# Unseen quarters left out of the scores on both PSUM banks, with a mask that clips first

## The chip, the cores and the metric

The kernel runs on one core of one Trainium2 chip. The metric is the device time of one execution in microseconds; three executions of the kernel before took 304.59, 306.55 and 308.75 us. Differences under 2% are called the same.

## The reference

Attention with a sliding window and a distance penalty (ALiBi), followed by a normalised two-layer MLP with a residual.

```python
# q, k, v: (8, 8, 576, 64) fp32
scores = q @ k.T / sqrt(64) - slope[h] * |i - j|      # slope[h] = 2 ** -(h + 1), 8 heads
mask   = (i - j >= 0) & (i - j < 128)                 # else -1e9
x      = softmax(scores) @ v                          # -> (8, 576, 512)
xn     = (x - mean(x)) / sqrt(var(x) + 1e-6) * g_ln
out    = x + relu(xn @ w_ch1) @ w_ch2                 # w_ch1 512x2048, w_ch2 2048x512
```

## The kernel before

**Tiling.** The eight batches are taken in four pairs p; a pair has nine blocks of 128 queries: blocks 0 to 7 are four blocks of each batch in turn, block 8 (T) holds the last 64 queries of both batches. That makes 36 blocks, numbered n = 9p + blk. The blocks are put into groups (four of 2 blocks, then seven of 4), and a group goes through the MLP at once.

**Attention of a block.** With a window of 128, a block of 128 queries sees its own keys and the 128 keys before them, `keys = [blk - 2, blk]`. `attend` (L472) does this for four heads at a time (`hps`, two pairs of heads), or for all eight where there is one block of keys. It multiplies in 64x64 tiles of TensorE: for each pair of heads and each block of keys, two halves of the keys (`c`) and two heads (`j`), 16 matmuls of up to 128 query columns (L498). ScalarE takes the exponential from PSUM into `probs` in 16 bits (L509); VectorE multiplies `probs` by a table `m_full` (or `m_ends`, `m_tail`) that holds the decay by distance and is zero outside of the window (`masks`, L531). The scores of a block are not shifted by their maximum.

**Unseen quarters.** Queries stand in PSUM with the even ones first, and half of the queries see none of one half of the keys' tile in a block: a quarter of the tile's columns is outside of the window. `seen` (L446) lists the column ranges to be multiplied: all of them if `all_of_it` (`full`), or in the first pair of batches for blocks under `SEEN` = 8; otherwise without the quarters, and for T only one batch's half (64 columns). Columns that are left out keep what the bank held, and the exponential runs over them too; the table's zeros then take them away.

**Banks.** Scores go to two PSUM places `ps_sc[0]` and `ps_sc[1]`, of two banks each. From block 12 on (`ONE_GO`) the two attends of a block are issued in one go, first onto `ps_sc[1]`, then onto `ps_sc[0]`. `values_at_once` (L586) writes the weighted values of a block, and the sums of its weights, into `ps_sc[1]` too. The sums come from a column of ones behind the values in `vext`. VectorE takes their reciprocal (L602) and multiplies (L603). In the kernel before, an attend onto `ps_sc[1]` from block 12 on has `full` set.

**The order of the work.** The order is written out by hand. `steps` is a list of small pieces of attention work; `weave_at` lets the MLP's units run and puts a given number of steps behind given units. All engines keep program order. From block 12 on a block has four steps: `go` (the two attends of block n + 2, with the exponential of the second put off), the masks that are left over, the values of block n and their centring (L635), then the put-off exponentials, then the masks of block n + 2 and the squares.

**The MLP.** `mlp1` (L858) has 16 units of four matmuls (L868) into one of four `ps_mm` banks; a Relu on ScalarE (L884), or for two of the units on VectorE (L876), writes the hidden tile. From group 4 on the second layer is `mlp2_seven` (L1085): seven products of half size in place of eight (Strassen's scheme), whose operands are sums of hidden tiles made on VectorE (`sum_hidden`, L1066; the subtractions stand on L918). It uses three banks x, t and y. Its products are issued in this order, each (L1098) with what VectorE or ScalarE then does:

| product | then |
|---|---|
| x, from the hidden tile | ScalarE copies x to t |
| y, from the first sum | `onto` the output (L1119) |
| onto x, from the second sum | `onto` (twice, for two blocks) |
| onto t, from the hidden tile | `onto` |
| onto x, from the third sum | `onto`; the product must wait until the `onto` before has read x |
| onto y, from the fourth sum | `onto`, store |
| onto x, from the hidden tile | `onto`, store |

The first sum is finished, the second made and the fourth begun while these run; VectorE does them between the masks and the values' normalising, in the order of the units.

**Loads** come on POOL's queue in the order of a list that `load_until` follows; stores and the transposing DMAs stand on SP's queue.

Of the kernel before, what the change touches and what calls it, by code (L numbers as in the profile page):

```python
# [14 lines left out]
ALU = mybir.AluOpType  # L15
# [14 lines left out]

FIRST_GROUPS, FIRST = 2, 4

BY_DMA = SEEN = 8

IN_HASTE = 10, 11

# [59 lines left out]
def kernel(  # L96
# [10 lines left out]
    nc = tc.nc  # L107
    B, H, S, D = q.shape
# [332 lines left out]
    weights_of, unmasked, scored, scored_only = {}, {}, [], []  # L441

    def in_halves(t):
        return t if len(t.shape) == 3 else t.rearrange("p (r c) -> p r c", r=2)

    def seen(p, blk, o, t, all_of_it):  # L446


        both, every = slice(0, 2), slice(0, HALF)
        first, second = slice(0, HALF // 2), slice(HALF // 2, HALF)  # L450
        if all_of_it or p == 0 and blk < SEEN:
            return [(0, both, every), (1, both, every)]
        if blk == T:
            batches = [slice(0, 1), slice(1, 2)]
            return [(c, batches[c if o == T else t], every) for c in range(2)]
        if o == blk:
            return [(0, both, every), (1, both, second)]
        return [(1, both, every), (0, both, first)]
# [10 lines left out]
                skip_group_check=True,  # L469
            )  # L470

    def attend(p, blk, keys, mask, tag, hps, sc=None, full=False, put_off=False):  # L472

        heads = slice(2 * hps[0], 2 * hps[-1] + 2)
        nk = len(keys)
        if hps[0] == 0:  # L480
            pr = probs_pool.tile([P, H, nk, P], FP16, tag=tag, name=tag)
            for t, o in enumerate(keys):
                weights_of.setdefault((p, blk), []).append((pr, t, o))
        else:
            pr = weights_of[p, blk][-1][0]
        banks = ps_sc[len(scored) % 2 if sc is None else sc]
        scored.append((p, blk))
        ps = banks.rearrange("p j (n t q) -> p j n t q", n=len(hps), t=nk)
        added = p == 0 and blk < ADDED
        qt, b = turned["q", p, blk // 2], blk % 2  # L490
        for n, hp in enumerate(hps):
            for t, o in enumerate(keys):
                kt = turned["k", p, o // 2][:, o % 2]
                for c, r, queries in seen(p, blk, o, t, full):
                    cols = slice(c * HALF, (c + 1) * HALF)
                    for j in range(2):
                        rows = slice(j * HALF, (j + 1) * HALF)
                        nc.tensor.matmul(  # L498
                            in_halves(ps[cols, j, n, t, :])[:, r, queries],
                            kt[rows, hp, cols],  # L500
                            in_halves(qt[rows, b, hp])[:, r, queries],
                            start=not added,
                            stop=True,
                            skip_group_check=added,
                        )
        dst = pr[:, heads].rearrange("p h t q -> p h (t q)")

        def weights():
            nc.scalar.activation(  # L509
                out=dst.rearrange("p (n j) q -> p j n q", j=2),  # L510
                in_=ps.rearrange("p j n t q -> p j n (t q)"),
                func=AF.Exp,
                scale=inv_sqrt_d,
            )

        if put_off:
            scored_only.append(weights)
        else:
            weights()
        if not added:  # L520
            unmasked.setdefault((p, blk), []).append((dst, mask[:, heads, :]))

    def exps():

# [2 lines left out]

    def masks(p, blk, n=3):
        todo = unmasked.get((p, blk), [])
        for dst, mask in todo[:n]:  # L530
            nc.vector.tensor_tensor(out=dst, in0=dst, in1=mask, op=ALU.mult)  # L531
        del todo[:n]

# [16 lines left out]
    def scores_tail(p):  # L550
        attend(*tail_attend(p))
# [3 lines left out]
    def values(p, blk, hg):  # L555

        if hg == 0:
            xs[p, blk] = x_pool.tile([P, DM], FP16, tag="x", name="x")
            sums[p, blk] = small.tile([P, 2], FP32, tag="sum", name="sum")
        ps = ps_mm.tile([P, 4, D + 1], FP32, tag="mm", name="ps_pv")  # L560
        terms = weights_of[p, blk]
        for i in range(4):
            h = 4 * hg + i
            for n, (pr, t, o) in enumerate(terms):
                nc.tensor.matmul(  # L565
                    ps[:, i, :],
                    pr[:, h, t, :],
                    vext[(p * NSLOT + o) % NV][:, h, :],
                    start=(n == 0),
                    stop=(n == len(terms) - 1),  # L570
                )
        rec = small.tile([P, 4], FP32, tag="rec", name="rec")
        nc.vector.reciprocal(out=rec, in_=ps[:, :, D])
        nc.vector.scalar_tensor_tensor(
            out=xs[p, blk][:, hg * 4 * D : (hg + 1) * 4 * D].rearrange(
                "p (h d) -> p h d", h=4
            ),
            in0=ps[:, :, 0:D],
            scalar=1.0,
            in1=rec.unsqueeze(2).broadcast_to([P, 4, D]),  # L580
            op0=ALU.mult,
            op1=ALU.mult,
            accum_out=sums[p, blk][:, hg : hg + 1],
        )

    def values_at_once(p, blk, sc=0):  # L586

        x = xs[p, blk] = x_pool.tile([P, DM], FP16, tag="x", name="x")
        total = sums[p, blk] = small.tile([P, 2], FP32, tag="sum", name="sum")
        ps = ps_sc[sc].rearrange("p g (h e) -> p (g h) e", h=4)  # L590
        terms = weights_of[p, blk]
        for h in range(H):
            for n, (pr, t, o) in enumerate(terms):
                nc.tensor.matmul(  # L594
                    ps[:, h, 0 : D + 1],
                    pr[:, h, t, :],
                    vext[(p * NSLOT + o) % NV][:, h, :],
                    start=(n == 0),
                    stop=(n == len(terms) - 1),
                )  # L600
        rec = small.tile([P, H], FP32, tag="rec8", name="rec8")
        nc.vector.reciprocal(out=rec, in_=ps[:, :, D])  # L602
        nc.vector.scalar_tensor_tensor(  # L603
            out=x.rearrange("p (h d) -> p h d", h=H),
            in0=ps[:, :, 0:D],
            scalar=1.0,
            in1=rec.unsqueeze(2).broadcast_to([P, H, D]),
            op0=ALU.mult,
            op1=ALU.mult,
            accum_out=total[:, 0:1],  # L610
        )
# [5 lines left out]
    def centre(p, blk):  # L617

        total = sums.pop((p, blk))
        mean = small.tile([P, 1], FP32, tag="mean", name="mean")  # L620
        if FIRST <= p * NSLOT + blk < BY_DMA:
            nc.vector.tensor_scalar(
# [17 lines left out]
        if at == 0:  # L640
            turned_x[g] = group_pool.tile([P, NKB, 4 * P], FP16, tag="xT", name="xT")
        if n < BY_DMA or g >= SEVEN:
            centred[p, blk] = xc
        if n >= BY_DMA and n not in IN_HASTE:
            nc.sync.dma_start_transpose(
# [72 lines left out]
    for g, size in enumerate(GROUPS):  # L718
        n = sum(GROUPS[:g])
# [20 lines left out]
    def x_step(n, copy=nc.vector.tensor_copy):  # L740
        return [(turn_x,) + home[n] + order[n] + (copy,)] if n < BY_DMA or n in IN_HASTE else []

# [44 lines left out]
    for n in range(8, ONE_GO):  # L787
        ahead = place[min(n + AHEAD, count - 1)]
        todo = []
# [12 lines left out]
        for tag, m in (("q", n + 5), ("k", n + 6)):  # L802
            if m < count and order[m][1] % 2 == 0 and by_dma(*order[m]):
                p, blk = order[m]
# [4 lines left out]
        steps += [step, second, third, fourth]  # L809

    for n in range(ONE_GO, count):
        todo = []
        if n + 1 < count and order[n + 1][1] == T:
            todo.append(tail_attend(order[n][0]))
        if n + 2 < count:
            todo += attends(*order[n + 2])
        first_of, pairs = n == ONE_GO, (1, 0) if len(todo) > 1 else (0,)
        go = [(attend, *a, sc, first_of or sc == 1, sc == 0) for a, sc in zip(todo, pairs)]  # L820
        step = [(load_until, place[min(n + AHEAD, count - 1)]), (masks,) + order[n]]
        step += [(values_at_once, *order[n], 1), (centre,) + order[n]]

        rest = [(masks, *args[:2], 1) for args in todo]
        rest += [(square, m) for m in {1: (), 3: (n - 2, n)}.get(n % 4, (n,))]
        for tag, m in (("q", n + 5), ("k", n + 6)):
            if m < count and order[m][1] % 2 == 0:
                p, blk = order[m]
                (step if first_of else rest).append((turn_natural, tag, p, blk // 2))
        steps += [go, step, [(exps,)], rest]  # L830
# [456 lines left out]
    for n, vx in enumerate(vext):  # L1287
        if n == 2:
            nc.vector.memset(ones, 1.0)
        nc.vector.memset(vx[:, :, D : D + 1], 1.0)  # L1290
    nc.vector.memset(magic, 0x5F3759DF)
    engine = mybir.EngineType
    with tc.manual_schedule(engines={engine.PE}):
# [64 lines left out]
```

## Time and profile before

| | |
|---|---|
| three executions | 304.59, 306.55, 308.75 us |
| the profiled one | 304.59 us; span from first to last instruction 302.8 us |
| granted TensorE clock, mean | 0.994 |
| TensorE matmuls | 294.7 us busy, 97% of the span, 3778 instructions |
| VectorE | 232.3 us, 77% |
| ScalarE | 184.4 us, 61% |
| GpSimd (loads) | 113.8 us, 38% |
| scores matmuls, L498 | 1088; 768 of 128 columns, 320 of 64 |
| masks, L531 | 66 of 128x1024 |

Busy time of TensorE counts overlapping, pipelined matmuls, so it is read together with the starts of the instructions. A row of instructions has the start in the span, the busy time, engine, line, operation, tiles written and read, shapes and count; in brackets the idle time before it and what ended that. A row of a group has busy time and mean of one in ns, then the idle time before, by what ended it. The chain of waits goes back from the last instruction to whatever released each; a row there has start, time, and engine, tile and line.

### The profile page before, as it was taken

How to read it: one execution, taken by the hardware profiler on the slowest of the kernel's cores; microseconds unless marked ns; L12 is line 12 of the kernel's file. 1: busy time of each engine (PE TensorE's matmuls, PEld its weight loads, DVE VectorE, ACT ScalarE, POOL GpSimd, SP SyncE). 2: the span in 40 equal slices, each digit the busy share in tenths (PEclk: the TensorE clock that was granted, in tenths of full speed). 3: DMA queues.
4: the chain of work that ended last, by engine and by line, in shares of the span. 5: the costliest groups of instructions: out<-in, count | busy, mean ns of one | idle time of the engine just before them, and what ended most of it. 6: DMA issues, size and time to landing. Idle time of an engine off the chain costs nothing.

```text
span 302.8 us, 9262 instructions
## 1 busy us (share of the span) xinstructions
PE 294.7 (97%) x3778; PEld 201.8 (67%) x3778; DVE 232.3 (77%) x616; ACT 184.4 (61%) x338; POOL 113.8 (38%) x153
## 2 busy tenths in 40 slices
PE   7899999999999999999999999999999999999994
PEld 2477755866855478556865686568656865788883
DVE  2588778779886788658866887687888888878983
ACT  5587777868967883478457745674577446606500
POOL 8933756973855571685007171760000000000000
PEclk9799999999999999999999999999999999999999
DMA  9999999999999999999979999999581153006014
GB/s 93 171 199 202 193 158 162 190 136 125 139 122 173 163 128 157 179 194 125 142 125 134 161 105 159 148 145 110 101 131 35 21 99 77 19 19 139 3 35 104
DMA packets 150074, 38.03 MB, mean 126 GB/s; under 512 B 140656, under 2 KB 145920, under 8 KB 150032
## 3 DMA queue, kind: packets, MB, share of 16 engines
q0 software_dynamic: 103792, 18.46, 89.1%
q1 hardware_dynamic: 45760, 18.60, 40.2%
q8 instruction: 29, 0.48, 0.7%
q10 hardware_dynamic: 480, 0.39, 0.5%
q14 instruction: 13, 0.11, 0.1%
HBM read 36.90 MB, written 9.44 MB: 153 GB/s over the span
## 4 chain that ended last, share of the span: by engine, by line
PE 88%; DMA 5%; DVE 3%; ACT 1%; issue 1%; POOL 1%; DVEq 0%; ACTq 0%; POOLq 0%
PE ps_m L868 35%; PE ps_s L1098 22%; PE ps_m L898 9%; PE ps_sc L498 5%; PE ps_sc L594 5%; PE ps_q L1176 4%; PE ps_x L992 3%; DMA q<-q 3%; DMA first<-in_k_dram 2%; PE ps_warm L334 1%; PE ps_tr L346 1%; DVE probs L531 1%; POOL first L190 1%; PE ps_pv L565 1%; PE ps_tx L655 1%
## 5 line engine op out<-in xcount | busy, mean ns | idle before, releaser
L868 PE MATMUL ps_m<-xT,w1g 128*128 128x512 f16 (+1 forms) x512 | 103.9, 353 | 0.2
L884 ACT ACTIVATE ht_all<-ps_m 128x512 f16<-128x512 f32 (+1 forms) x143 | 71.8, 512 | 37.9 <-PE ps_m L868 36.0
L868 PEld LDWEIGHTS <-w1g 128*128 128x128 f16 x512 | 47.6, 98 | 41.7 <-issue 0.6
L509 ACT ACTIVATE probs<-ps_sc 128x1024 f16<-128x1024 f32 x56 | 56.1, 1022 | 9.4 <-PE ps_sc L498 9.4
L289 POOL DMA_DIRECT2D vx<-in_v_dram x40 | 35.3, 893 | 65.1 <-PE ps_sc L594 47.2
L1098 PE MATMUL ps_s<-w,s 128*128 128x256 f16 x384 | 45.7, 273 | 0.1
L1098 PEld LDWEIGHTS <-s 128*128 128x128 f16 x384 | 36.8, 98 | 4.4 <-issue 0.2
L531 DVE TENSOR_TENSOR probs<-probs,m 128x1024 f16<-128x1024 f16 x56 | 36.3, 685 | 1.8 <-ACT probs L509 1.8
L1098 PE MATMUL ps_s<-w,ht_all 128*128 128x256 f16 x288 | 36.1, 273 | 0.0
L679 ACT ACTIVATE junk<-xc 128x512 f16<-128x512 f16 x28 | 17.7, 631 | 26.9 <-DVE xc L635 26.9
L898 PE MATMUL ps_m<-w,ht_all 128*128 128x512 f16 x128 | 31.5, 380 | 0.0
L1098 PEld LDWEIGHTS <-ht_all 128*128 128x128 f16 x288 | 27.3, 98 | 5.0
L278 POOL DMA_DIRECT2D q<-in_q_dram x40 | 27.5, 701 | 6.0 <-DMA vx<-in_v_dram 5.3
L918 DVE TENSOR_TENSOR s<-ht_all 128x1024 f16<-128x1024 f16 (+2 forms) x36 | 20.5, 570 | 11.6 <-ACT ht_all L884 10.6
L498 PEld LDWEIGHTS <-k 64*64 64x64 f16 x1088 | 15.8, 107 | 13.1 <-issue 11.7
L603 DVE SCALAR_TENSOR_TENSOR x<-ps_sc,rec 128x512 f16<-128x512 f32 x32 | 22.1, 692 | 1.2 <-DVE rec L602 0.2
L1119 DVE SCALAR_TENSOR_TENSOR o<-ps_s,rstd,x 128x256 f32<-128x256 f32 x48 | 20.9, 477 | 2.6 <-PE ps_s L1098 2.2
L498 PE MATMUL ps_sc<-q,k 64*64 64x128 f16 (+1 forms) x1088 | 21.6, 213 | 0.9 <-DVE k L420 0.4
L275 POOL DMA_DIRECT2D k<-in_k_dram x20 | 17.9, 911 | 6.1 <-DMA k<-k 4.9
L602 DVE RECIPROCAL rec<-ps_sc 128x8 f32<-128x8 f32 x32 | 6.5, 204 | 17.2 <-PE ps_sc L594 17.2
L594 PEld LDWEIGHTS <-probs 128*128 128x128 f16 x384 | 15.9, 98 | 3.7
L898 PEld LDWEIGHTS <-ht_all 128*128 128x128 f16 x128 | 11.0, 98 | 10.6
(118 smaller groups left out, 377.1 us busy)
## 6 DMA issues: line engine op xcount, KB each, us to landing
out_dram<-o SPq DMA_DIRECT2D x64, 128.0 KB, 3.4
vx<-in_v_dram POOLq DMA_DIRECT2D x32, 128.0 KB, 7.3
w<-in_moe_w_ch_dram POOLq DMA_DIRECT2D x8, 512.0 KB, 11.3
k<-in_k_dram POOLq DMA_DIRECT2D x30, 128.0 KB, 6.9
q<-in_q_dram POOLq DMA_DIRECT2D x48, 64.0 KB, 6.6
q<-in_q_dram POOLq DMA_DIRECT2D x10, 128.0 KB, 6.0
out_dram<-o SPq DMA_DIRECT2D x10, 64.0 KB, 2.0
k<-in_k_dram POOLq DMA_DIRECT2D x8, 64.0 KB, 7.3
```

What stands on the lines that cost most here:

```text
L278: nc.gpsimd.dma_start(out=t[half, b], in_=tokens.rearrange("h (c r) d -> r c h d", r=2)[r],)
L289: nc.gpsimd.dma_start(out=vx[p0 : p0 + n, :, 0:D], in_=v[b, :, t0 : t0 + n, :].rearrange("h p d -> p h d"),)
L498: nc.tensor.matmul(in_halves(ps[cols, j, n, t, :])[:, r, queries], kt[rows, hp, cols], in_halves(qt[rows, b, hp])[:, r, queries], start=no ...
L509: nc.scalar.activation(out=dst.rearrange("p (n j) q -> p j n q", j=2), in_=ps.rearrange("p j n t q -> p j n (t q)"), func=AF.Exp, scale=in ...
L531: nc.vector.tensor_tensor(out=dst, in0=dst, in1=mask, op=ALU.mult)
L594: nc.tensor.matmul(ps[:, h, 0 : D + 1], pr[:, h, t, :], vext[(p * NSLOT + o) % NV][:, h, :], start=(n == 0), stop=(n == len(terms) - 1),)
L603: nc.vector.scalar_tensor_tensor(out=x.rearrange("p (h d) -> p h d", h=H), in0=ps[:, :, 0:D], scalar=1.0, in1=rec.unsqueeze(2).broadcast_t ...
L868: nc.tensor.matmul(ps[:, 0:cols], w[:, kb, fb * P : (fb + 1) * P], xT[:, kb, 0:cols], start=(kb == 0), stop=(kb == NKB - 1),)
L884: nc.scalar.activation(out=ht[:, fb, :], in_=ps[:, 0:cols], func=AF.Relu)
L898: nc.tensor.matmul(sums[at], ht[:, fb, at * P : (at + 1) * P], w2[:, fb, :], start=(fb == 0), stop=(fb == NFB - 1),)
L1098: nc.tensor.matmul(ps[:, pair, :], lhs[:, fb, at : at + P], rhs[:, fb, :], start=(first and pair == 0 and fb == 0), stop=(fb == half - 1), ...
L1119: nc.vector.scalar_tensor_tensor(out=outs[at][:, cols], in0=ps[:, pair], scalar=rstd[:, n : n + 1], in1=(xs[p, blk] if fresh else outs[at] ...
```

## The change

The quarters are left out on `ps_sc[1]` also after values were written there, and in the first pair of batches for blocks 3, 5 and 7. What such a column then holds after the exponential can be past the range of 16 bits (infinite), and infinite times zero is no number; so for these attends (`values_were`) the mask first takes the smaller of the weight and 65504 and then multiplies. The ones behind the values become 2 to the -7, so that the sums left in the bank stay small, and the scaling of the values has the same factor. `full` remains for the one attend on `ps_sc[0]` of block 12's go.

```diff
-BY_DMA = SEEN = 8
+BY_DMA = 8
+ONE = 2.0**-7
+ALL_SEEN = 0, 1, 2, 4, 6
...
-        if all_of_it or p == 0 and blk < SEEN:
+        if all_of_it or p == 0 and blk in ALL_SEEN:
             return [(0, both, every), (1, both, every)]
...
-    def attend(p, blk, keys, mask, tag, hps, sc=None, full=False, put_off=False):
+    def attend(p, blk, keys, mask, tag, hps, sc=None, full=False, put_off=False, values_were=False):
...
-            unmasked.setdefault((p, blk), []).append((dst, mask[:, heads, :]))
+            unmasked.setdefault((p, blk), []).append((dst, mask[:, heads, :], values_were))
...
-        for dst, mask in todo[:n]:
+        for dst, mask, values_were in todo[:n]:
+            if values_were:
+                nc.vector.scalar_tensor_tensor(
+                    out=dst, in0=dst, scalar=65504.0, in1=mask, op0=ALU.min, op1=ALU.mult
+                )
+                continue
             nc.vector.tensor_tensor(out=dst, in0=dst, in1=mask, op=ALU.mult)
...
-            scalar=1.0,
+            scalar=ONE,
...
-        go = [(attend, *a, sc, first_of or sc == 1, sc == 0) for a, sc in zip(todo, pairs)]
+        go = [
+            (attend, *a, sc, first_of and sc == 0, sc == 0, sc == 1) for a, sc in zip(todo, pairs)
+        ]
...
-        nc.vector.memset(vx[:, :, D : D + 1], 1.0)
+        nc.vector.memset(vx[:, :, D : D + 1], ONE)
```

`scalar=ONE` stands in `values` and in `values_at_once`.

More of the change, by code (lines that the diff above doesn't have):

```diff
@@ L605, in values_at_once @@
             in0=ps[:, :, 0:D],
-            scalar=1.0,
+            scalar=ONE,
             in1=rec.unsqueeze(2).broadcast_to([P, H, D]),
```

## The prediction

> **What bounds the kernel now.** I read the page first, then a table by stretches of the span, then the chain of waits, then the rows of TensorE (PE) and VectorE (DVE) one by one around each place where the chain left PE.
>
> ```profile
> span 302.8 us, 9262 instructions
> PE 294.7 (97%) x3778; PEld 201.8 (67%) x3778; DVE 232.3 (77%) x616; ACT 184.4 (61%) x338; POOL 113.8 (38%) x153
> PE 88%; DMA 5%; DVE 3%; ACT 1%; issue 1%; POOL 1%; DVEq 0%; ACTq 0%; POOLq 0%
> core 0: us, PE busy (x) PEld busy (x) DVE busy (x) ACT busy (x) POOL busy (x), PEclk, DMA share, GB/s
> 154.00:185.00 31.00, 31.00 (x373) 20.91 (x372) 23.48 (x61) 19.00 (x31) 12.57 (x16) 1.00 1.46 136
> ```
>
> The first line is the span. The second and third say that the kernel is bound by PE: busy for 97% of the span, and 88% of the chain that ended last lies on it. The stretch 154 to 185 us is one whole group of four blocks: PE is busy throughout at the full clock, DVE for 23.5 of 31 us. DVE looks as if it had a quarter of its time to spare. But 3% of the chain is DVE, and the change puts work on DVE, so the question is where those 3% lie. The chain between 139 and 150 us answers it:
>
> ```profile
> 139.81 0.61 ACT ht_all L884
> 140.42 0.02 issue
> 140.44 0.44 DVE s L918
> ...
> 140.90 0.83 DVE s L918
> 141.73 1.21 DVE probs L531 x2
> 142.93 0.41 DVE s L918
> ...
> 146.20 1.28 DVE probs L531 x2
> 147.48 0.80 DVE o L1119 x2
> 148.28 0.04 issue
> 148.32 1.69 PE ps_s L1098 x14
> ```
>
> When the last Relu of `mlp1` is done (139.81 + 0.61), DVE starts a queue without a gap: two sums of the hidden tile, two masks (`probs` L531), the long sum, the block's normalising (`rec`, `x`), the results `onto` the output, two more masks, and the `onto` that empties bank x. PE's product at L1098, which accumulates into that same bank, waits for that last one and starts 0.04 us after it. Both mask pairs stand inside this queue. So in this stretch each added DVE nanosecond is a PE nanosecond.
>
> **The change, part by part.**
>
> *Matmuls of the scores.* Nothing is added to PE; in the built program 248 matmuls of L498 have 64 columns where they had 128: 21 attends of 16 matmuls have 8 of them halved, and 5 (those of the tail blocks) all 16. The trace has all these forms side by side, since the attend on bank 0 already leaves the quarters out:
>
> ```profile
> 37.46 0.64 PE L498 MATMUL ps_sc<-q,k 64*64 64x128 f16 x32
> 38.03 0.39 PE L898 MATMUL ps_m<-w,ht_all 128*128 128x512 f16 x1
> ...
> 97.41 0.59 PE L498 MATMUL ps_sc<-q,k 64*64 64x128 f16 x32
> 97.94 0.39 PE L868 MATMUL ps_m<-xT,w1g 128*128 128x512 f16 x1
> ...
> 109.58 0.54 PE L498 MATMUL ps_sc<-q,k 64*64 64x128 f16 x32
> 110.05 0.39 PE L1098 MATMUL ps_s<-w,ht_all 128*128 128x256 f16 x2
> ```
>
> From the first matmul of a pair of attends to the next work: full and full, 38.03 - 37.46 = 0.57 us; full and a quarter less, 97.94 - 97.41 = 0.53; full and tail, 110.05 - 109.58 = 0.47. An attend with 8 halved is 0.05 cheaper, a tail one 0.10. In all 21 x 0.05 + 5 x 0.10 = 1.55 us of PE, at the very most.
>
> *Masks.* In the built program 20 of the 66 masks (18 `probs`, 2 `own` with `m_tail`) turn from a TENSOR_TENSOR into a SCALAR_TENSOR_TENSOR with two operations. One in each pair of L531 changes, the first. Nothing else on DVE, ScalarE, POOL or SP moves, and the order of every queue stays. The trace has no SCALAR_TENSOR_TENSOR on 16-bit data of this size, so I bound it by the nearest rows:
>
> ```profile
> L531 DVE TENSOR_TENSOR probs<-probs,m 128x1024 f16<-128x1024 f16 x56 | 36.3, 685 | 1.8 <-ACT probs L509 1.8
> L603 DVE SCALAR_TENSOR_TENSOR x<-ps_sc,rec 128x512 f16<-128x512 f32 x32 | 22.1, 692 | 1.2 <-DVE rec L602 0.2
> L574 DVE SCALAR_TENSOR_TENSOR x<-ps_pv,rec 128x256 f16<-128x256 f32 x8 | 3.4, 424 | 0.3
> L918 DVE TENSOR_TENSOR ps_s<-ps_x,c 128x512 f32<-128x512 f32 x4 | 2.8, 694 | 0.5 <-PE ps_x L992 0.5
> L918 DVE TENSOR_TENSOR s<-ht_all 128x512 f16<-128x512 f16 x10 | 4.3, 425 | 4.8 <-ACT ht_all L884 4.5
> L1119 DVE SCALAR_TENSOR_TENSOR o<-ps_s,rstd,x 128x256 f32<-128x256 f32 x48 | 20.9, 477 | 2.6 <-PE ps_s L1098 2.2
> ```
>
> A TENSOR_TENSOR in 16 bits goes from 425 ns (512 elements) to 685 (1024): 0.51 ns an element. The 32-bit one at 512 takes 694. The SCALAR_TENSOR_TENSOR goes from 424 (256) to 692 (512): 1.05 ns an element, with 156 ns fixed. Low end: the new mask keeps the 16-bit rate, 0.685 us, nothing added. High end: the slope of 1.05 and the fixed part of L1119 (477 - 256 x 1.05 = 208), 1.28 us. I take the rows of the same instruction, 156 + 1024 x 1.05 = 1.23 us, so +0.545 us for each of the 20. The one doubt is that those rows read 32-bit data from PSUM.
>
> [...]
>
> *What of it lies on the path.* In the stages of `mlp1` the added time meets idle time of DVE; the next row after such masks is
>
> ```profile
> 162.39 1.28 DVE L531 TENSOR_TENSOR probs<-probs,m 128x1024 f16<-128x1024 f16 x2
> 163.59 0.68 DVE L918 TENSOR_TENSOR s<-ht_all 128x1024 f16<-128x1024 f16 x1
> 166.12 0.56 DVE L918 TENSOR_TENSOR s<-ht_all 128x768 f16<-128x768 f16 x1 [1.84 <-ACT ht_all L884]
> ...
> 173.50 0.49 PE ps_sc L594 x16
> ```
>
> 1.84 us idle, of which 0.545 is used up: nothing (were that cover gone, 0.545 us late onto the sums). The masked weights themselves are read two blocks later, by the values matmuls at 173.50 (last row, from the chain), so they are never late.
>
> In the second half of each of groups 4 to 8 (`mlp2_seven`) there is no idle time between the last Relu and the emptying of bank x. End of that `onto` against PE's start:
>
> ```profile
> 116.83 0.87 DVE L1119 SCALAR_TENSOR_TENSOR o<-ps_s,rstd,x 128x256 f32<-128x256 f32 x2
> 117.77 0.38 PE L1098 MATMUL ps_s<-w,s 128*128 128x256 f16 x2
> ...
> 177.88 0.87 DVE L1119 SCALAR_TENSOR_TENSOR o<-ps_s,rstd,x 128x256 f32<-128x256 f32 x2
> 178.80 0.38 PE L1098 MATMUL ps_s<-w,s 128*128 128x256 f16 x2
> ...
> 202.72 0.69 DVE L531 TENSOR_TENSOR own<-own,m 128x1024 f16<-128x1024 f16 x1
> 207.88 0.87 DVE L1119 SCALAR_TENSOR_TENSOR o<-ps_s,rstd,x 128x256 f32<-128x256 f32 x2
> 209.19 0.38 PE L1098 MATMUL ps_s<-w,s 128*128 128x256 f16 x2
> ...
> 238.51 0.87 DVE L1119 SCALAR_TENSOR_TENSOR o<-ps_s,rstd,x 128x256 f32<-128x256 f32 x2
> 239.45 0.38 PE L1098 MATMUL ps_s<-w,s 128*128 128x256 f16 x2
> ```
>
> Taking 0.05 us from a DVE end to a PE start, the slack is 0.02 (117.77), none (148.32, where PE already waits), none (178.80), 0.39 (209.19), 0.02 (239.45). Four of these queues hold two changed masks, 2 x 0.545 = 1.09 us; that of 209.19 holds one, because the first place there is an `own` mask of bank 0 that does not change. The stalls: 1.07 + 1.09 + 1.09 + 0.15 + 1.07 = 4.47 us. What is late next: product x with the third sum, and through it the rest of PE's queue. DVE itself recovers behind it, as it next waits for PE there.
>
> *What PE keeps of its saving.* Attends between the last Relu and the waiting product save nothing, for the product starts when DVE says. That is two pairs in each of the five queues: 0.20 (a tail block's two attends) + 0.10 + 0.15 + 0.10 + 0.10 = 0.65 us. Of the six changed attends of the first batches, the two of block 3 and the two of block 5 run just before PE waits for ScalarE's or DVE's results: another 0.20. There remain 1.55 - 0.65 - 0.20 = 0.70 us.
>
> *No cost:* memsets of 2 to the -7 and the constant in the two scalings have the instructions, shapes and places they had.
>
> Sum: +4.47 - 0.70 = +3.8 us against the profiled execution's 304.59 us (span 302.8 and 1.8 around it): 308.4. That execution was the fastest of the three shown; on their median of 306.55 it is 310.3, a ratio of 1.012. I give 310.3.
>
> **The rivals.**
>
> *A. The mask keeps its rate.* If the engine takes two 16-bit results at a time here too, 0.685 us, no queue grows and only the matmuls count: the saving is 0.70, and some 0.15 more in the queue of 209.19, which has slack: 0.85 us less, 305.7. For it: the same operands run at 0.51 ns an element in L531. Against it: each row of this instruction has 1.05. It decides from the mask's duration: nine changed masks stand in the five queues, so the gain of 0.70 is eaten at about 0.08 us each; under 0.77 us the change is not slower.
>
> [...]
>
> *C. The cover in the `mlp1` stages fails too.* DVE also empties two PSUM banks of `mlp1` in each group (L876) in the same queue. If these come late enough for PE to run out of banks, up to two more changed masks per group count: 5 x 2 x 0.545 = +5.5 on top, 316. Against it: the 1.84 us idle above and four banks. It decides from where the idle time behind the masks is below 0.5 us.
>
> *That the matmuls don't shrink* is excluded by the built program and the 0.53 us row.
>
> **How the numbers follow.** Forecast 0.76, A 0.12, B 0.05, C 0.07. The likeliest one's own range: masks from 1.1 to 1.28 us give +2.7 to +4.4, and the three runs shown spread by 2 us to each side: 307.5 to 313. To hold 8 in 10 with A on the low side I give 304.8 to 313.5; B and C are left out. About what a measurement of this kernel can tell from no change is 2%, 6.1 us: 300.4 to 312.7. Over it lie B, C and a small part of the forecast: 0.15; under it hardly anything, since A reaches 305.7: 0.02; within: 0.83.
>
> **What would show it.** In the changed profile: the new form of the mask at about 1230 ns x18; DVE's busy time up by some 11 us to 243; pairs of L498 at 0.47 to 0.48 us before the next work; PE's product at L1098 starting about 1.1 us later behind each last `onto` in four groups; DVE's share of the chain up from 3% to some 10%, all in the second halves of the groups. I am wrong if the mask is at 0.69 us (A) or over 2 us (B), if the five queues got idle time, or if PE waits in the `mlp1` stages for L876 (C).

## The result and the profile after

The changed kernel took 309.63 us (median of six, 308.49 to 310.33) against 306.23 us for the kernel before: a ratio of 1.0107, with a 95% interval of 1.0066 to 1.0149. It is slower by 3.4 us; by the bound of 2% that counts as the same. Medians here and below are of all executions, while ratios and their 95% intervals leave out those more than 1.5% above the fastest of the same kernel, so the two can differ by a few tenths of a percent.

The page of the profiled execution (309.78 us), the lines that answer to those of before:

```profile
span 308.0 us, 9262 instructions
PE 292.9 (95%) x3778; PEld 200.1 (65%) x3778; DVE 244.9 (80%) x616; ACT 184.0 (60%) x338; POOL 112.6 (37%) x153
PE 75%; DVE 12%; DMA 4%; issue 3%; POOL 3%; ACT 1%; DVEq 0%; POOLq 0%
```

DVE has 12.6 us more to do, and its share of the chain that ended last went from 3% to 12%. The 20 longer masks are 10.6 us of that; most of the rest lies in rows that the change does not touch (the centring 13.5 to 14.8 us, the scaled weights `w1g` 4.6 to 5.6). Lines of the file are 12 further down at the end (L1131 is the `onto` that was L1119, L1110 the product that was L1098). The masks, grouped by shape:

```profile
L542 DVE TENSOR_TENSOR probs<-probs,m 128x1024 f16<-128x1024 f16 x38 | 25.4, 685 | 1.6 <-ACT probs L514 1.6
L538 DVE SCALAR_TENSOR_TENSOR probs<-probs,m 128x1024 f16<-128x1024 f16 x18 | 21.9, 1217 | 0.0
```

The clipping mask takes 1217 ns where the plain one takes 685: 0.53 us more. Less the 156 ns that the prediction took as fixed, that is 1.04 ns an element. Next the chain of waits through the second half of one group, to be read beside the chain of before at 139 to 148 us:

```profile
173.46 0.61 ACT ht_all L896
174.06 0.02 issue
174.09 0.44 DVE s L930
...
175.37 1.14 DVE probs L538
176.51 0.60 DVE probs L542
...
180.52 1.13 DVE probs L538
181.65 0.38 DVE probs L542
182.03 0.14 issue
182.18 0.87 DVE o L1131 x2
183.05 0.04 issue
183.09 0.92 PE ps_s L1110 x7
```

From the Relu's end to the product the chain is DVE alone, with a long mask at two places. What PE waited for now, in total, times and longest (the list of waits, PE alone):

```profile
PE ps_s L1110 <- DVE o L1131: 4.4, 4, 1.2
PE ps_m L880 <- DMA w<-in_moe_w_ch_dram: 2.0, 1, 2.0
```

The same product in PE's rows, once for each of the five queues, with the idle time in brackets:

```profile
120.24 0.49 PE L1110 MATMUL ps_s<-w,s 128*128 128x256 f16 x3 [1.08 <-DVE o L1131]
...
151.58 0.60 PE L1110 MATMUL ps_s<-w,s 128*128 128x256 f16 x4 [1.21 <-DVE o L1131]
183.09 0.60 PE L1110 MATMUL ps_s<-w,s 128*128 128x256 f16 x4 [1.13 <-DVE o L1131]
213.52 0.70 PE L1110 MATMUL ps_s<-w,s 128*128 128x256 f16 x5
244.74 0.70 PE L1110 MATMUL ps_s<-w,s 128*128 128x256 f16 x5 [0.97 <-DVE o L1131]
```

Four waits, 4.4 us; the product at 213.52, in the queue with slack, has none. No such line stood in the list of waits before. The second line of the list is a load of weights that landed late at the start. The same matmuls after it, before and in the changed kernel:

```profile
24.54 0.40 PE L655 MATMUL ps_tx<-first_tables,xc 128*128 128x128 f16 x4 [0.47 <-DVE xc L635]
25.78 0.40 PE L666 MATMUL ps_tx<-first_tables,xc 128*128 128x128 f16 x4 [0.52 <-DVE xc L646]
```

So the changed kernel is 1.24 us late there, before any of the waits on DVE. That is the larger part of why the profiled spans differ by 5.2 us and the medians only by 3.4. The other side, PE's saving:

```profile
165.38 0.54 PE L503 MATMUL ps_sc<-q,k 64*64 64x128 f16 x32
165.85 0.82 PE L880 MATMUL ps_m<-xT,w1g 128*128 128x512 f16 x3
```

A pair of attends is past after 0.47 us in place of 0.53.

### The profile page after: what moved, and what is told of

It is laid out like the page before. It is cut to its first block, busy times and chain, and to the rows that moved or that the text cites. A ratio compares the mean times of both kernels' runs of the same rounds, so it can differ in the third digit from the quotient of the medians.

```text
span 308.0 us, 9262 instructions
## 1 busy us (share of the span) xinstructions
PE 292.9 (95%) x3778; PEld 200.1 (65%) x3778; DVE 244.9 (80%) x616; ACT 184.0 (60%) x338; POOL 112.6 (37%) x153
## 4 chain that ended last, share of the span: by engine, by line
PE 75%; DVE 12%; DMA 4%; issue 3%; POOL 3%; ACT 1%; DVEq 0%; POOLq 0%
PE ps_m L880 35%; PE ps_s L1110 13%; PE ps_m L910 9%; PE ps_q L1188 4%; PE ps_sc L605 4%; DMA w<-in_moe_w_ch_dram 3%; PE ps_sc L503 3%; PE ps_x L1004 3%; DVE s L930 3%; DVE probs L538 3%; DVE o L1131 2%; DVE x L614 2%; DVE probs L542 1%; POOL vx L294 1%; ACT ht_all L896 1%
## 5 line engine op out<-in xcount | busy, mean ns | idle before, releaser
L880 PE MATMUL ps_m<-xT,w1g 128*128 128x512 f16 (+1 forms) x512 | 103.9, 353 | 0.3 <-DVE o L1253 0.3
L880 PEld LDWEIGHTS <-w1g 128*128 128x128 f16 x512 | 47.7, 98 | 41.6 <-issue 0.5
L294 POOL DMA_DIRECT2D vx<-in_v_dram x40 | 34.2, 865 | 73.0 <-PE ps_sc L605 61.5
L1110 PE MATMUL ps_s<-w,s 128*128 128x256 f16 x384 | 45.7, 272 | 4.5 <-DVE o L1131 4.4
L1110 PEld LDWEIGHTS <-s 128*128 128x128 f16 x384 | 36.8, 98 | 9.4 <-issue 5.3
L1110 PE MATMUL ps_s<-w,ht_all 128*128 128x256 f16 x288 | 36.1, 273 | 0.0
L1110 PEld LDWEIGHTS <-ht_all 128*128 128x128 f16 x288 | 27.4, 98 | 5.0
L542 DVE TENSOR_TENSOR probs<-probs,m 128x1024 f16<-128x1024 f16 x38 | 25.4, 685 | 1.6 <-ACT probs L514 1.6
L503 PEld LDWEIGHTS <-k 64*64 64x64 f16 x1088 | 14.4, 107 | 13.3 <-issue 11.9
L538 DVE SCALAR_TENSOR_TENSOR probs<-probs,m 128x1024 f16<-128x1024 f16 x18 | 21.9, 1217 | 0.0
L1131 DVE SCALAR_TENSOR_TENSOR o<-ps_s,rstd,x 128x256 f32<-128x256 f32 x48 | 20.5, 476 | 1.2 <-PE ps_s L1110 0.8
L503 PE MATMUL ps_sc<-q,k 64*64 64x128 f16 (+1 forms) x1088 | 20.2, 207 | 1.0 <-issue 0.5
L605 PEld LDWEIGHTS <-probs 128*128 128x128 f16 x384 | 15.9, 98 | 3.7 <-issue 0.2
```

Of the source, the lines that this page charges most:

```text
L294: nc.gpsimd.dma_start(out=vx[p0 : p0 + n, :, 0:D], in_=v[b, :, t0 : t0 + n, :].rearrange("h p d -> p h d"),)
L503: nc.tensor.matmul(in_halves(ps[cols, j, n, t, :])[:, r, queries], kt[rows, hp, cols], in_halves(qt[rows, b, hp])[:, r, queries], start=no ...
L538: nc.vector.scalar_tensor_tensor(out=dst, in0=dst, scalar=65504.0, in1=mask, op0=ALU.min, op1=ALU.mult)
L605: nc.tensor.matmul(ps[:, h, 0 : D + 1], pr[:, h, t, :], vext[(p * NSLOT + o) % NV][:, h, :], start=(n == 0), stop=(n == len(terms) - 1),)
L880: nc.tensor.matmul(ps[:, 0:cols], w[:, kb, fb * P : (fb + 1) * P], xT[:, kb, 0:cols], start=(kb == 0), stop=(kb == NKB - 1),)
L1110: nc.tensor.matmul(ps[:, pair, :], lhs[:, fb, at : at + P], rhs[:, fb, :], start=(first and pair == 0 and fb == 0), stop=(fb == half - 1), ...
```

## The experiments

The theory under test: the change costs the added length of the clipping mask, and only where the mask stands in the queue between the last Relu and the `onto` that empties bank x; the shorter matmuls save a little. Rival 1: the matmuls of 64 columns, or the exponential over values, cost. Rival 2: DVE's load as such costs, wherever it lies. Rival 3 came with the remedy: the wait only moves on to the next bank. The first four kernels split the change into its parts.

**The change with the old mask.** Nothing clips at 65504 here.

```diff
-            if values_were:
+            if False:
```

> The change with the old mask everywhere: quarters left out and the ones at 2 to the -7 as in the change, but every mask a plain TENSOR_TENSOR (no clipping at 65504). Queue theory (what costs is the longer mask where it stands between the last Relu and the emptying of bank x): only the shorter matmuls are left, 0.85 us less than before, some 305.4 us against 306.2; no wait of PE for L1131's onto above 0.2 us. Rival 1 (the cost is in the matmuls of 64 columns, or in the exponential over columns that hold values): stays some 3 us above before. Rival 2 (DVE's total load): as the queue theory here.

Measured: 305.04 us against 306.11, ratio 0.9964 (0.9931 to 0.9998). Rival 1 falls: the part with the matmuls is a gain, and the size forecast (0.85 us would be 0.9972) lies in the interval. The list of waits still has one on the `onto` at L1131, of 0.3 us, a little over the 0.2 us expected. The profiled execution also waited 2.2 us for a transposing DMA (1.6 us in the kernel that clips only outside of the queues, further down); neither the profile before nor that of the changed kernel has this wait, and why it came stays open.

**The mask alone.** All quarters are multiplied, the same 20 masks clip.

```diff
-ALL_SEEN = 0, 1, 2, 4, 6
+ALL_SEEN = 0, 1, 2, 3, 4, 5, 6, 7
...
-            (attend, *a, sc, first_of and sc == 0, sc == 0, sc == 1) for a, sc in zip(todo, pairs)
+            (attend, *a, sc, first_of or sc == 1, sc == 0, sc == 1) for a, sc in zip(todo, pairs)
```

> The other part alone: all quarters multiplied as before, but the same 20 masks clip first. Queue theory: the stalls alone, 4.47 us, so some 310.7 us against 306.2 (ratio 1.0146). Rival 1 (the matmuls cost): within 0.5 us of before. Rival 2 (DVE's total load): +4 us too, not told apart here.

Measured: 310.22 us, ratio 1.0135 (1.0105 to 1.0164), 4.1 us more than before. The mask alone accounts for the whole loss. Its list of waits:

```profile
PE ps_s L1110 <- DVE o L1131: 3.9, 4, 1.1
```

**Clipping only outside of the queues.** The nine masks in the queues don't clip.

```diff
-            if values_were:
+            if values_were and not ((p * NSLOT + blk) % 4 < 2 and mask.shape[1] == 4):
```

> The change, but only the 11 masks outside of the five queues clip (blocks n with n mod 4 = 2 or 3 and the two tails); the nine in the queues are plain. DVE's load is up by 11 x 0.53 = 5.9 us. Queue theory: no stall, 0.85 us less than before, 305.4 us. Rival 2 (each added DVE time costs a like share wherever it stands): 11/20 of 4.2 less 0.85, so 1.5 us more than before, 307.7 us.

Measured: 304.61 us, ratio 0.9950 (0.9926 to 0.9974). "No stall" holds but for one wait on L1131, of 0.4 us at 150.74, in the queue in which PE already waited before the change.

**Clipping only in the queues.** The other eleven don't clip.

```diff
-            if values_were:
+            if values_were and (p * NSLOT + blk) % 4 < 2 and mask.shape[1] == 4:
```

> The change, but only the nine masks in the five queues clip; DVE's load is up by 9 x 0.53 = 4.8 us. Queue theory: all stalls of the change, so its whole 3.4 us over before, 309.6 us. Rival 2: 9/20 of 4.2 less 0.85, 1.0 us over before, 307.3 us.

Measured: 309.11 us, ratio 1.0110 (1.0075 to 1.0144). The page's line of the kernel that clips outside of the queues, that of the one that clips inside, and the latter's list of waits:

```profile
PE 292.7 (96%) x3778; PEld 199.7 (66%) x3778; DVE 238.8 (78%) x616; ACT 184.2 (60%) x338; POOL 113.4 (37%) x153
```

```profile
PE 291.8 (95%) x3778; PEld 199.6 (65%) x3778; DVE 237.7 (77%) x616; ACT 184.0 (60%) x338; POOL 112.8 (37%) x153
```

```profile
PE ps_s L1110 <- DVE o L1131: 4.4, 4, 1.2
```

The kernel with more work on DVE (238.8 us) is the faster one; the one with less (237.7) has all of the loss, 3.0 of 3.4 us, and the same 4.4 us of waits as the change. Rival 2 falls: it wanted 307.7 and 307.3. The place of the mask decides.

**The whole change, second mask pair behind the `onto`.** All 20 masks clip; one number in the order of the steps differs.

```diff
-    TWICE = [1, 4, 5, 7, 7, 11, 12], [0, 0, 5, 5, 8, 12, 19, 19, 23]
+    TWICE = [1, 4, 5, 7, 7, 11, 12], [0, 0, 5, 5, 11, 12, 19, 19, 23]
```

> The change whole, with its clipping masks; only the second mask pair of each mlp2_seven is issued after unit 11 in place of 8, that is behind the onto that empties bank x. Queue theory: the queue from the last Relu to that onto loses 1.13 + 0.6 us and keeps one longer mask, so it is some 0.75 us shorter than before the change: no stalls, and the shorter matmuls now count there too: 1.55 less 0.20 lost early, and the 0.2 us stall of before gone: 1.5 us less than before, some 304.6 us. Rival 2 (DVE's load): +3 us as in the change. Rival 3 (the wait moves on to the next onto, that of bank t, and through it to the next product): between 305 and 309 us, with PE waiting for L1131 some 1 us later in each group.

Measured: 304.71 us against 304.87, ratio 0.9966 (0.9926 to 1.0006). The loss is gone; a gain is likely but not shown. DVE's rows in the same half group, PE's row, the page's line and the list of waits:

```profile
178.34 1.64 DVE L1131 SCALAR_TENSOR_TENSOR o<-ps_s,rstd,x 128x256 f32<-128x256 f32 x4
179.91 1.21 DVE L538 SCALAR_TENSOR_TENSOR probs<-probs,m 128x1024 f16<-128x1024 f16 x1
181.04 0.68 DVE L542 TENSOR_TENSOR probs<-probs,m 128x1024 f16<-128x1024 f16 x1
181.64 0.86 DVE L1131 SCALAR_TENSOR_TENSOR o<-ps_s,rstd,x 128x256 f32<-128x256 f32 x2
```

```profile
180.48 1.91 PE L1110 MATMUL ps_s<-w,s 128*128 128x256 f16 x16
```

```profile
PE 293.5 (97%) x3778; PEld 201.0 (66%) x3778; DVE 243.4 (80%) x616; ACT 183.7 (60%) x338; POOL 112.4 (37%) x153
```

```profile
PE ps_tr L419 <- DMA first<-in_k_dram: 2.8, 2, 2.3
PE ps_warm L339 <- DVE vx L1302: 1.5, 1, 1.5
PE ps_m L880 <- DMA xT<-xc: 1.0, 1, 1.0
```

The `onto` of bank y and that of bank x (two instructions each) now run at 178.34 to 179.98, before the masks, and the product at 180.48 follows with half a microsecond in hand. No wait on L1131 is left, so rival 3 falls too, while DVE is almost as busy as in the change (243.4 and 244.9 us). The waits that remain are on loads and on DVE's first work at the start, and on a transposing DMA.

**The kernel before with the same move.**

> The kernel before with the same move of the second mask pair and nothing else. Queue theory: the queues had almost no slack but only one real stall of 0.2 us, so 0.2 to 0.3 us less than before, not told from the same: 305.9 us. Rival 3: 0.5 to 1 us more.

Measured: 305.26 us, ratio 1.0011 (0.9980 to 1.0042): no difference that can be told. The move does not make the kernel faster by itself; it takes away the loss.

**The old mask with the same move.**

> The change with plain masks everywhere and the same move. Queue theory: as with the clipping masks moved, since neither has a stall: within 0.3 us of it, some 304.5 us. If the longer mask costs in other places too, this one is faster by more.

Measured: 303.75 us, ratio 0.9954 (0.9917 to 0.9990). Its ratio lies 0.1% from that of the clipping one with the move (0.9966), inside both intervals: a cost of clipping, once the second mask stands behind the `onto`, is not shown. With intervals of this width a cost of half a percent could hide.

**The mask in bfloat16**, for its duration alone.

```diff
-                    out=dst, in0=dst, scalar=65504.0, in1=mask, op0=ALU.min, op1=ALU.mult
+                    out=dst.bitcast(BF16), in0=dst.bitcast(BF16), scalar=65504.0, in1=mask.bitcast(BF16), op0=ALU.min, op1=ALU.mult
```

> The change with the operands of the clipping mask read and written as bfloat16 (same bytes, so its values mean nothing; for the duration alone). [...] If the instruction takes one element a time in either type, 1.22 us again; so I expect it, from the slope of the 32-bit rows of the same instruction.

```profile
L539 DVE SCALAR_TENSOR_TENSOR probs<-probs,m 128x1024 bf16<-128x1024 bf16 x18 | 21.9, 1217 | 0.0
```

The mask takes 1217 ns in either type.

**More of the same.** The second mask of each `probs` pair in the queues clips too, nine more.

```diff
-            if values_were:
+            if values_were or p and (p * NSLOT + blk) % 4 < 2 and p * NSLOT + blk > 15 and mask.shape[1] == 4:
```

> The change, and in the five queues the second mask of each probs pair clips too: nine more long masks, all in queues (two more in four of them, one more in that at 209 us, whose slack is used up by then). Queue theory: each lengthens a queue by 0.53 us and PE by as much, 9 x 0.53 = 4.8 us more than the change, 314.4 us. If DVE catches up somewhere between (a stall once paid covers the next), less than 3 us more; if late masks begin to hold the mlp1 stages as well (rival C of the prediction), more than 6.

Measured: 319.29 us against 305.50, ratio 1.0462 (1.0430 to 1.0495): 13.8 us more than before, so 10.4 us on top of the change's 3.4, twice what was expected. Expected was also that more than 6 us would point to rival C of the prediction; but its list of waits has no line for the matmuls of `mlp1` (L880). The wait on L1131 in that list, and PE's rows at the four longest (the fifth, of 0.60 us, is in the queue that had slack):

```profile
PE ps_s L1110 <- DVE o L1131: 9.4, 5, 2.3
```

```profile
120.61 0.60 PE L1110 MATMUL ps_s<-w,s 128*128 128x256 f16 x4 [2.14 <-DVE o L1131]
153.00 2.96 PE L1110 MATMUL ps_s<-w,s 128*128 128x256 f16 x16 [2.27 <-DVE o L1131]
187.35 1.02 PE L1110 MATMUL ps_s<-w,s 128*128 128x256 f16 x6 [2.34 <-DVE o L1131]
252.22 3.17 PE L1110 MATMUL ps_s<-w,s 128*128 128x256 f16 x16 [2.04 <-DVE o L1131]
```

Two windows of four microseconds there (PE's granted clock is the third number from the right), and the product as a piece of the chain, at the first wait and at the third:

```profile
150.00:154.00 4.00, 1.73 (x15) 1.35 (x14) 3.73 (x6) 1.75 (x2) 0.00 (x0) 0.96 1.50 171
154.00:158.00 4.00, 4.00 (x37) 3.25 (x35) 1.86 (x6) 0.00 (x0) 0.88 (x1) 0.61 0.00 0
```

```profile
120.61 1.91 PE ps_s L1110 x16
...
187.35 3.16 PE ps_s L1110 x16
```

The waits grew from 4.4 to 9.4 us: 5.0, as the queue theory has it (9 x 0.53 = 4.8). The rest fits the clock. Behind the first wait the 16 matmuls of a product take 1.91 us; behind those at 153, 187 and 252 us they take 2.96 to 3.17, and the granted clock falls to 0.61 of full speed in the four microseconds after 154. From 0.96 and 0.61 over four microseconds each, 0.16 + 1.56 = 1.7 us of clock are lost there. In the chain that ended last the product and the 48 matmuls behind it (16 of L605, 32 of L1110) take 1.91 + 0.49 + 3.49 = 5.89 us at the first wait, and 2.96 + 0.88 + 3.68 = 7.52, 3.16 + 0.87 + 3.49 = 7.52 and 3.17 + 0.85 + 3.49 = 7.51 us at those at 153, 187 and 252 us: 1.6 us more each, 4.9 us in all. 5.0 + 4.9 = 9.9 us, against the 10.4 measured. Over the whole span of 317.1 us the granted clock is 0.978, so 7.0 us are lost, against 1.8 us before (0.994 of 302.8 us). No run holds the clock fixed, so this part is a sum that fits, not an experiment.

## Why the prediction was right

- *What bounds.* PE bounds, and DVE's masks are on the path only in the second halves of the groups: shown by the pair of kernels that clip inside and outside of the queues.
- *The mask's duration.* 1.23 us taken, 1.217 measured: 1.04 ns an element, near the 1.05 of the 32-bit rows of this instruction and twice the 0.51 of the plain mask. A is out. No run shows a mask of over 2 us, the term behind B's 0.05: in each run that clips, the clipping masks took 1206 to 1217 ns (means by form), and with the bfloat16 operands 1210 and 1217.
- *The stalls.* 1.07, 1.09, 1.09 and 1.07 forecast for the queues with two long masks; PE's rows have 1.08, 1.21, 1.13 and 0.97, 4.39 together against 4.32. That they agree so closely is in part luck: the forecast is the time added, the bracket is all idle time. A second measure is the time from one group's waiting product to the next group's, which takes in what PE saves: from before (117.77 to 239.45) to the change (120.24 to 244.74) the four distances grew by 0.79, 1.03, 0.04 and 0.96, 2.82 us together. The forecast for them is 1.09 + 1.09 + 0.15 + 1.07 = 3.40, less their part of the 0.70 that PE keeps. So the size holds, to some tenths. The queue with slack grew by 0.04; forecast was a stall of 0.15, and no wait is listed there.
- *PE's saving.* Forecast 0.70 kept. The kernel with the old mask is 0.4% below the one before (0.85 us would be 0.3%; the interval goes from 0.02% to 0.7%), so a saving is shown, its size only roughly. The change against the kernel with the mask alone (ratios 1.0107 and 1.0135) points the same way, but the intervals overlap. The rows that the prediction used give 0.04 us for an attend with a quarter less (0.57 - 0.53), not 0.05; the pair in the changed kernel is 0.06 shorter (0.53 to 0.47).
- *The sum.* +3.8 forecast, +3.4 measured. The 0.4 between is inside the interval of the ratio and is not traced further. The prediction's own range for masks of 1.1 to 1.28 us comes out at +2.6 to +4.2 us when worked again, not +2.7 to +4.4; the measured +3.4 lies in either.
- *Rival C* (masks of the `mlp1` stages hold PE) is out: the eleven long masks outside of the queues cost nothing that shows, and no list of waits has PE's matmuls of `mlp1` behind a Relu of DVE.
- *What could have misled:* the profiled spans differ by 5.2 us, 1.8 more than the medians. PE was 1.24 us late after the load of weights, before the first of the five queues; the profile of the kernel with the mask alone has 0.9 us of that wait in place of 2.0, so its length goes by the execution.

## What to carry to other kernels

An engine that is busy for 77% can still have stages without any slack; ask of each added instruction which queue it stands in, and what the engine that bounds the kernel waits for at the end of that queue. Fusing a second operation into an elementwise instruction need not be free: here the fused form took 1217 ns and the plain one 685 on the same 16-bit tile. Where the order is written by hand, moving the longer instruction behind the one that the other engine waits for can take the loss away, as one changed number did here.

## What was not expected of the hardware

A wait of PE of 2.04 to 2.34 us can cost more than its length: in the last kernel above, the 64 matmuls behind it took 1.6 us longer at three of the four waits above 2 us (2.27, 2.34 and 2.04, but not 2.14). Behind the wait of 2.27 us, over at 153.00, the granted clock was 0.61 from 154 to 158 us; behind that of 2.14 us it was 1.00 from 120 to 132 us. The four waits on DVE of the changed kernel, up to 1.21 us, had no such tail, nor had its wait of 1.96 us for the weights: its granted clock is 0.999 over the span. A wait for a DMA can have the tail too. This is the change with the old mask, with its wait for the transposing DMA and what came behind it:

```profile
126.02 2.40 PE L880 MATMUL ps_m<-xT,w1g 128*128 128x512 f16 x8 [2.25 <-DMA xT<-xc]
```

```profile
126.00:128.00 2.00, 1.99 (x8) 0.75 (x8) 0.54 (x4) 0.60 (x1) 1.66 (x2) 0.81 3.79 122
128.00:130.00 2.00, 2.00 (x20) 0.83 (x20) 0.00 (x0) 0.60 (x1) 0.11 (x1) 0.50 1.94 153
130.00:132.00 2.00, 2.00 (x9) 0.85 (x8) 0.00 (x0) 0.90 (x2) 0.00 (x0) 0.84 1.36 294
```

The granted clock is 0.81, 0.50 and 0.84 over two microseconds each, so 0.38 + 1.00 + 0.32 = 1.7 us are lost again. The length of one wait does not decide by itself: 2.04 us was followed by a loss and 2.14 us was not. Nor is a long wait needed: the profile before lost 1.7 us between 10 and 14 us (granted clock 0.50 and 0.64 over two microseconds each), where no wait of PE in the four microseconds before was over 0.6 us, though PE was busy for just 2.7 of them.
